# Grouping the attention work of chunks 4 to 7 into pairs, and four slices of the second token group on 512 tokens

## The chip, the core and the metric

One core of a Trainium2 chip runs the kernel. The metric is the device time of one execution in microseconds (us). The engines are named as in the profile: PE (TensorE: matmuls, and PEld its weight loads), DVE (VectorE), ACT (ScalarE), POOL (GpSimd), SP (SyncE, which here only issues transfers).

## What is computed

Sliding-window causal attention (window 64, 8 batches, 8 heads, 576 tokens, head size 64), whose output goes through a gated feed-forward block:

```
scores = scale * q @ k^T ; mask = (0 <= rel < 64) ; attn = softmax(scores)
x = (attn @ v), reshaped to 4608 tokens x 512
out = (silu(x @ w_gate) * (x @ w_val)) @ w_out      # 512 -> 1536 -> 512
```

## The kernel before

**Tiling.** The 4608 tokens are 36 chunks of 128 tokens and 9 groups of 512 tokens (four chunks each). A chunk's attention is three steps. Scores: PE multiplies keys and queries (64-row matmuls, lines 661 and 665), ACT takes the exponential into `pt` (line 673), and DVE multiplies by the window's mask (`Sm`, lines 723 and 725). AV: PE multiplies `pt` with the values, which carry a column of ones, so that the row sums come out as well. Normalization: DVE takes reciprocals of the sums (line 807) and multiplies (line 810) into `xb`. Then `xb` is transposed to `xT`: for the early chunks by PE (line 980) with a copy from PSUM by ACT or DVE (`X`), later by a DMA on SP.

**The feed-forward part.** A group of 512 tokens has 12 slices F of 128 hidden units. A slice is four matmuls with `Wg` and four with `Wv` (line 1055), a tanh on ACT (`sig`, line 1062) and two DVE operations (`uu`, line 1064, and `hT`, line 1066). Behind the 12 slices stand four outputs O (12 matmuls each with `Wo`, line 1087; ACT copies the result out of PSUM). A slice can also be made of halves: `F1.0-1a` is slices 0 and 1 of group 1 on its first 256 tokens, `F1.10a` slice 10 alone on these; `b` is the second 256 tokens. The first 256 tokens need the `xT` of two chunks, a slice on 512 tokens that of four.

**Two forms of AV.** A query block of 64 tokens needs the keys of its own and of the preceding 64-token block. The form A (`AVs`, line 791) contracts over 128 rows in one matmul. For that, the values of the two key blocks must lie on the 128 partitions in the right halves; for every chunk but the first this takes a copy `vs` of values whose halves are put in by two copies, `H` or `h` (`shift`; 64 rows each, on ACT or POOL). There are three `vs` buffers; `VS` names the buffer of each chunk (chunk 3 has buffer 2, and so have chunks 4 and 6; chunk 5 has buffer 1, chunk 7 buffer 0). The form B (`AVmm`, line 762) contracts over 64 rows and needs no copy; the word `B4` in the order puts the scores of chunk 5 between the two halves of chunk 4's AV and then adds the normalization of chunk 4 and the mask of chunk 5.

**The order.** It is written out by hand. `EARLY` is the order of the work up to group 2; each word records operations, and each engine executes its own in the order of recording. A dependency on another engine becomes a semaphore wait in front of the instruction, behind which that engine's queue stands still. The words: `F`, `O`, `X` as above; `k2t`, `q3t`: PE transposes the keys or queries of two chunks, ACT (for half of k2t DVE) copies them out; `S4`: scores, exponentials and mask; `S4u`: the same without the mask, which the word `m4` records later; `A5`: AV in form A; `N5`: its normalization; `H4.1.1/act`: copy half 1 of the values of chunk 4 into buffer 1, on ACT. `LOADS` is the order of the DMAs that POOL issues, with POOL's own copies (`h6.1.0`) among them; a word of it is recorded as soon as its `ready` condition holds, and stops all words behind it until then. `SHIPS` is the order on SP. PSUM has eight banks; the recorder gives each step the free bank that by its own estimate is ready first.

In the kernel before, chunks 4 to 7 go so: S4 | F0.8 | B4 (with S5) | F0.9 | X4, k3t, A5 | F0.10 | X5, q3t | F0.11 | S6 | two slice pairs | B6 (with S7) | two slice pairs | X6, A7 | slices 8 to 10 on 256 tokens | X7 | slice 11 on 256 tokens, and then the second 256 tokens of group 1, with S8 and S9 in one block, and O0.0.

Of the kernel before, what the change touches and what calls it, by code (L numbers as in the profile page):

```python
# [32 lines left out]
class _Graph:  # L33
# [13 lines left out]
    def ready(self, k):  # L47
        return max((o.end for o in self.writers.get(k, []) + self.readers.get(k, [])), default=0.0)
# [294 lines left out]
class _Kernel:  # L343
# [14 lines left out]

    VS = (0, 0, 1, 2, 2, 1, 2, 0)
    EARLY = """  # L360
        V F0.4 F0.5 F0.6 k2t q2t F0.7 S4 F0.8 H4.1.1/act H5.0.1/act B4 F0.9 X4/act k3t A5 N5 F0.10 X5/act q3t F0.11 S6
        F1.0-1a F1.2-3a B6 F1.4-5a F1.6-7a X6/act A7 N7 F1.8-9a F1.10a X7/act F1.11a F1.0-1b F1.2-3b F1.4-5b F1.6-7b
        S8 S9 F1.8-9b F1.10-11b O0.0 O0.1 P8 m10 O0.2 m11 O0.3 P10 m12 O1.0 X10/act X11/act m13 O1.1 F2.0 F2.1 F2.2
        F2.3 F2.4 P12 F2.5 m14 F2.6 m15 F2.7 O1.2 P14 F2.8 m16 F2.9 m17 F2.10 F2.11 O1.3 K O2.0
    """
    LOADS = """
        k2.2 q2.2 Wg8-10 Wv8-10 v4 v5 k3.2 Wg10-12 Wv10-12 q3.2 v6 v7 k8 q8 k9 q9 Wo0-6 k10 q10 k11 q11 Wo6-12 v8 h6.1.0
        h7.0.0 v9 k12 q12 k13 q13 v10 v11 k14@O0.2 q14 k15 q15 v12 v13 k16 q16 k17 q17 v14 k18 q18 v15 k19 q19 q20 v16
        v17 k20@F2.9 q21@F2.9 k21@F2.9 q22@F2.9 v18@F2.9 v19@F2.9 k22@F3.4 q23@F3.4 k23@F3.4 q24@F3.4 v20@F3.4 v21@F3.4
        k24@O2.3 q25@O2.3 k25@O2.3 q26@O2.3 v22@O2.3 v23@O2.3 k26@O3.1 q27@O3.1 k27@O3.1 q28@O3.1 v24@O3.1 v25@O3.1  # L370
        k28@O3.3 q29@O3.3 k29@O3.3 q30@O3.3 v26@O3.3 v27@O3.3 k30@O4.1 q31@O4.1 k31@O4.1 q32@O4.1 v28@O4.1 v29@O4.1
# [790 lines left out]
    def ready(self, t):  # L1162

        d = self.did
        w, n = t[0], int(re.search(r"\d+", t).group())
        if w == "W":
            return True
        if w in "kq" and t.endswith(".2"):
            return n < 2 or w + "%dT" % (n - 2) in d
        if w in "kq":  # L1170
            return n < 16 or "T%s%d" % (w, n - 8) in d
        if w == "v":
            return n < self.NV or {"a%d" % (n - self.NV), "a%d" % (n - self.NV + 1)} <= d
        if w == "h":
            return {"v%d" % n, "V"} | ({"a3"} if t in ("h5.1.2", "h6.0.2") else set()) <= d
        if w == "x":
            c = n // 4
            return "a%d" % n in d and (c < self.NX or self.steps[c - self.NX] == NF * 512)
        x = t[1]
        return x + "%d" % n in d and (n < 8 or {"s%d" % (n - 8), "s%d" % max(0, n - (9 if x == "q" else 7))} <= d)  # L1180
# [279 lines left out]
```

## Time and profile before

| | us |
|---|---|
| three runs, median (lowest, highest) | 328.25 (326.68, 329.33) |
| profiled execution, own time | 327.04 |
| profiled execution, span | 325.2 |
| PE busy in the span | 315.4 (97%) |
| DVE, ACT, POOL busy | 205.3, 135.9, 109.8 |

A row of a timeline reads: start in us, duration in us (for several merged instructions from the first start to the last end), engine, line, operation, what it writes and reads, the tile of the array that a matmul uses, shapes, how often, and in brackets the idle time of that engine just before with the engine that ended it. Matmuls are pipelined: one issues 0.2 us after another, though each is given a longer duration; so the time of a group is read from its start to the start of the next group. Some records are missing in a trace: where a row of four matmuls shows "x3", its first start is one matmul too late.

### The profile page before, as it was taken

How to read it: one execution, taken by the hardware profiler on the slowest of the kernel's cores; microseconds unless marked ns; L12 is line 12 of the kernel's file. 1: busy time of each engine (PE TensorE's matmuls, PEld its weight loads, DVE VectorE, ACT ScalarE, POOL GpSimd, SP SyncE). 2: the span in 40 equal slices, each digit the busy share in tenths (PEclk: the TensorE clock that was granted, in tenths of full speed). 3: DMA queues.
4: the chain of work that ended last, by engine and by line, in shares of the span. 5: the costliest groups of instructions: out<-in, count | busy, mean ns of one | idle time of the engine just before them, and what ended most of it. 6: DMA issues, size and time to landing. Idle time of an engine off the chain costs nothing.

```text
span 325.2 us, 8029 instructions
## 1 busy us (share of the span) xinstructions
PE 315.4 (97%) x3417; PEld 170.2 (52%) x3452; DVE 205.3 (63%) x360; ACT 135.9 (42%) x244; POOL 109.8 (34%) x138
## 2 busy tenths in 40 slices
PE   7899999999999999999999999999999999999996
PEld 6585578855455445545444454545454544444443
DVE  4678978745387737665757575766656564854610
ACT  3734864534445236343434342525252522322322
POOL 8899990007930702406060607070502000000000
PEclk9999999999999999999999999999999999999999
DMA  9999999999999994969998999999996200201012
GB/s 139 180 186 168 170 174 134 141 136 128 147 155 154 106 171 107 145 149 155 160 164 147 163 130 126 135 120 127 125 120 80 67 34 32 69 34 38 32 64 100
DMA packets 165563, 39.93 MB, mean 123 GB/s; under 512 B 152848, under 2 KB 160784, under 8 KB 165520
## 3 DMA queue, kind: packets, MB, share of 16 engines
q0 software_dynamic: 115152, 18.62, 80.6%
q1 hardware_dynamic: 45040, 11.22, 25.9%
q10 hardware_dynamic: 5328, 9.51, 8.3%
q8 instruction: 29, 0.48, 0.6%
q14 instruction: 14, 0.11, 0.1%
HBM read 37.75 MB, written 9.44 MB: 145 GB/s over the span
## 4 chain that ended last, share of the span: by engine, by line
PE 93%; ACT 2%; DMA 2%; issue 1%; DVE 0%; POOLq 0%
PE ps L1055 57%; PE ps L1087 28%; PE ps L840 2%; DMA qs<-in_q_dram 2%; ACT pt L673 2%; PE ps L698 1%; PE ps L661 1%; PE ps L1120 1%; ACT pt L710 1%; PE ps L980 1%; PE ps L605 1%; PE ps L665 1%; PE ps L791 0%; PE ps L608 0%; PE ps L702 0%
## 5 line engine op out<-in xcount | busy, mean ns | idle before, releaser
L1055 PE MATMUL ps<-xT,Wv 128*128 128x512 bf16 (+1 forms) x487 | 110.5, 351 | 0.5
L1055 PE MATMUL ps<-xT,Wg 128*128 128x512 bf16 (+1 forms) x478 | 107.5, 351 | 2.6 <-issue 1.4
L1064 DVE SCALAR_TENSOR_TENSOR uu<-sig,ps 128x512 bf16<-128x512 bf16 (+1 forms) x109 | 74.0, 679 | 53.4 <-ACT sig L1062 52.5
L1062 ACT ACTIVATE sig<-ps 128x512 bf16<-128x512 f32 (+1 forms) x109 | 64.9, 597 | 80.5 <-PE ps L1055 79.3
L1087 PE MATMUL ps<-Wo,hT 128*128 128x512 bf16 x413 | 94.5, 379 | 0.6 <-ACT pt L673 0.3
L1066 DVE SCALAR_TENSOR_TENSOR hT<-uu,ps 128x512 bf16<-128x512 bf16 (+1 forms) x109 | 74.3, 682 | 3.8
L1055 PEld LDWEIGHTS ps<-xT,Wv 128*128 128x128 bf16 x496 | 48.5, 98 | 44.9
L551 POOL DMA_DIRECT2D kn<-in_k_dram x31 | 29.4, 953 | 123.6 <-PE ps L1087 94.0
L1055 PEld LDWEIGHTS ps<-xT,Wg 128*128 128x128 bf16 x496 | 46.6, 98 | 41.6 <-ACT pt L673 0.2
L1087 PEld LDWEIGHTS ps<-Wo,hT 128*128 128x128 bf16 x420 | 40.9, 98 | 48.7
L1094 ACT ACTIVATE ost<-ps 128x512 f32<-128x512 f32 x35 | 20.9, 597 | 89.1 <-PE ps L1087 83.1
L551 POOL DMA_DIRECT2D va<-in_v_dram x40 | 36.2, 964 | 12.3 <-PE ps L1087 12.3
L551 POOL DMA_DIRECT2D qn<-in_q_dram x31 | 29.7, 969 | 0.0
L867 DVE RECIPROCAL rr<-ps 128x14 f32<-128x14 f32 (+1 forms) x28 | 5.7, 204 | 36.1 <-PE ps L840 35.9
L673 ACT ACTIVATE pt<-ps 128x512 bf16<-128x512 f32 x36 | 18.8, 598 | 4.8 <-PE ps L665 4.6
L869 DVE TENSOR_TENSOR xb<-ps,rr 128x896 bf16<-128x896 f32 (+1 forms) x28 | 19.4, 691 | 1.0
L710 ACT ACTIVATE pt<-ps 128x512 bf16<-128x512 f32 x36 | 18.6, 603 | 2.3 <-PE ps L702 2.1
L840 PEld LDWEIGHTS ps<-va,pt 64*64 64x64 bf16 x888 | 10.8, 107 | 6.1 <-issue 5.9
L840 PE MATMUL ps<-va,pt 64*64 64x65 bf16 x888 | 13.4, 193 | 0.1
L725 DVE TENSOR_TENSOR pt<-pt,kmask 128x1024 bf16<-128x1024 bf16 x18 | 12.3, 684 | 0.0
L725 DVE TENSOR_TENSOR pt<-pt,mask 128x1024 bf16<-128x1024 bf16 x13 | 8.8, 686 | 0.8 <-ACT pt L673 0.8
L1130 DVE COPY ost<-ps 128x128 f32<-128x128 f32 x1 | 0.3, 293 | 11.8 <-PE ps L1120 11.8
(75 smaller groups left out, 151.7 us busy)
## 6 DMA issues: line engine op xcount, KB each, us to landing
out_dram<-ost ACTq DMA_DIRECT2D x35, 256.0 KB, 3.0
va<-in_v_dram POOLq DMA_DIRECT2D x32, 128.0 KB, 6.7
kn<-in_k_dram POOLq DMA_DIRECT2D x25, 128.0 KB, 5.4
qn<-in_q_dram POOLq DMA_DIRECT2D x25, 128.0 KB, 5.5
Wg<-in_moe_w_gate_dram POOLq DMA_DIRECT2D x6, 256.0 KB, 7.4
Wv<-in_moe_w_val_dram POOLq DMA_DIRECT2D x6, 256.0 KB, 7.4
Wo<-in_moe_w_out_dram POOLq DMA_DIRECT2D x2, 768.0 KB, 18.9
qs<-in_q_dram POOLq DMA_DIRECT2D x3, 256.0 KB, 6.9
```

What stands on the lines that cost most here:

```text
L551: self.g.op("pool", lambda e, d=d, a=a: e.dma_start(d, a), writes=ks, dma=True, after=self.hold)
L673: g.op("act", lambda e, po=po, p=p: e.activation(po, sv[p], ACTF.Exp, scale=SCALE), reads=[bx[p][1]], writes=[pk[p]])
L710: g.op("act", lambda e, po=po, p=p: e.activation(po, sv[p], ACTF.Exp, scale=SCALE), reads=[bx[p][1]], writes=[pk[p]])
L725: self.g.op("dve", lambda e: e.tensor_tensor(pt, pt, m, ALU.mult), reads=pk + [key], writes=pk)
L840: z = e.matmul(self.psa[64 * c:64 * c + 64, o:o + 65], pt[p][rows, h, 64 * a:64 * a + 64], va[m][rows, h, 0:65], start=first, stop=phase = ...
L869: g.op("dve", lambda e, d=d, num=num, rb=rb: e.tensor_tensor(d, num, rb, ALU.mult), reads=bk + [("rr", n + k)], writes=xk, cost=(1.0, 0.25 ...
L1055: r = e.matmul(bank[:, a * n:a * n + n], W[:, kk, f * 128:f * 128 + 128], xT[:, kk, lo:hi], start=(kk == 0), stop=(kk == NK - 1))
L1062: g.op("act", lambda e, G=bank: e.activation(sig[:, 0:w], G[:, 0:w], ACTF.Tanh, scale=0.5), reads=[bk], writes=[("sig", i)])
L1064: g.op("dve", lambda e: e.scalar_tensor_tensor(uu[:, 0:w], sig[:, 0:w], 1.0, G[:, 0:w], ALU.add, ALU.mult), reads=[("sig", i), gk], writes ...
L1066: g.op("dve", lambda e: e.scalar_tensor_tensor(out, v3(uu), 0.5, v3(V), ALU.mult, ALU.mult), reads=[("uu", i), vk], writes=[("hT", ih, f) ...
L1087: r = e.matmul(OB[:, :], hT[:, f, 128 * u:128 * u + 128], self.Wo[:, f, :], start=(f == 0), stop=(f == NF - 1), skip_group_check=mid is no ...
L1094: g.op("act", lambda e: e.activation(ost[:, :], OB[:, :], ACTF.Copy), reads=[ok], writes=[("ost", io)])
```

## The change

Chunks 4 and 5, and then 6 and 7, are taken together. The scores of two chunks stand in one block (`S4u S5u`), their masks are recorded behind the slice that follows (`m4 m5` behind F0.8, `m6 m7` behind F1.0-1a), and their AVs, all in form A, stand in one block one slice later (`A4 A5 N4 N5`). X4 and X5 go together behind q3t, X5's copy moves from ACT to DVE, X6 and X7 go together in front of F1.8. Slices 8 to 11 of group 1 are taken on 512 tokens in place of two halves of 256. S8 and S9 keep their distance of two slice pairs from O0.0.

The form A of chunks 4 and 6 needs four more copies: h3.1.2 (POOL, between the loads of v5 and k3), H4.0.2 (ACT), and h5.1.2 and h6.0.2 (POOL). The last two stand, with h6.1.0 and h7.0.0, in front of the load of k10, and are recorded once `a4` is done, since they overwrite the buffer that A4 reads.

```diff
     EARLY = """
-        V F0.4 F0.5 F0.6 k2t q2t F0.7 S4 F0.8 H4.1.1/act H5.0.1/act B4 F0.9 X4/act k3t A5 N5 F0.10 X5/act q3t F0.11 S6
-        F1.0-1a F1.2-3a B6 F1.4-5a F1.6-7a X6/act A7 N7 F1.8-9a F1.10a X7/act F1.11a F1.0-1b F1.2-3b F1.4-5b F1.6-7b
-        S8 S9 F1.8-9b F1.10-11b O0.0 O0.1 P8 m10 O0.2 ...
+        V F0.4 F0.5 F0.6 k2t q2t F0.7 S4u S5u F0.8 H4.0.2/act H4.1.1/act H5.0.1/act m4 m5 F0.9 A4 A5 N4 N5 k3t F0.10 q3t
+        X4/act X5/dve F0.11 S6u S7u F1.0-1a m6 m7 F1.2-3a A6 A7 N6 N7 F1.4-5a F1.6-7a X6/act X7/act F1.8 F1.9 F1.10 F1.11
+        F1.0-1b F1.2-3b
+        S8 S9 F1.4-5b F1.6-7b O0.0 O0.1 P8 m10 O0.2 ...
     LOADS = """
-        k2.2 q2.2 Wg8-10 Wv8-10 v4 v5 k3.2 Wg10-12 Wv10-12 q3.2 v6 v7 k8 q8 k9 q9 Wo0-6 k10 q10 k11 q11 Wo6-12 v8 h6.1.0
-        h7.0.0 v9 k12 ...
+        k2.2 q2.2 Wg8-10 Wv8-10 v4 v5 h3.1.2 k3.2 Wg10-12 Wv10-12 q3.2 v6 v7 k8 q8 k9 q9 Wo0-6 h5.1.2 h6.0.2 h6.1.0 h7.0.0 k10
+        q10 k11 q11 Wo6-12 v8 v9 k12 ...
         if w == "h":
-            return {"v%d" % n, "V"} | ({"a3"} if t in ("h5.1.2", "h6.0.2") else set()) <= d
+            return {"v%d" % n, "V"} | ({"a4"} if t in ("h5.1.2", "h6.0.2") else set()) <= d
```

More of the change, by code (lines that the diff above doesn't have):

```diff
@@ L360 @@
     EARLY = """
-        V F0.4 F0.5 F0.6 k2t q2t F0.7 S4 F0.8 H4.1.1/act H5.0.1/act B4 F0.9 X4/act k3t A5 N5 F0.10 X5/act q3t F0.11 S6
-        F1.0-1a F1.2-3a B6 F1.4-5a F1.6-7a X6/act A7 N7 F1.8-9a F1.10a X7/act F1.11a F1.0-1b F1.2-3b F1.4-5b F1.6-7b
-        S8 S9 F1.8-9b F1.10-11b O0.0 O0.1 P8 m10 O0.2 m11 O0.3 P10 m12 O1.0 X10/act X11/act m13 O1.1 F2.0 F2.1 F2.2
+        V F0.4 F0.5 F0.6 k2t q2t F0.7 S4u S5u F0.8 H4.0.2/act H4.1.1/act H5.0.1/act m4 m5 F0.9 A4 A5 N4 N5 k3t F0.10 q3t
+        X4/act X5/dve F0.11 S6u S7u F1.0-1a m6 m7 F1.2-3a A6 A7 N6 N7 F1.4-5a F1.6-7a X6/act X7/act F1.8 F1.9 F1.10 F1.11
+        F1.0-1b F1.2-3b
+        S8 S9 F1.4-5b F1.6-7b O0.0 O0.1 P8 m10 O0.2 m11 O0.3 P10 m12 O1.0 X10/act X11/act m13 O1.1 F2.0 F2.1 F2.2
         F2.3 F2.4 P12 F2.5 m14 F2.6 m15 F2.7 O1.2 P14 F2.8 m16 F2.9 m17 F2.10 F2.11 O1.3 K O2.0
@@ L366 @@
     LOADS = """
-        k2.2 q2.2 Wg8-10 Wv8-10 v4 v5 k3.2 Wg10-12 Wv10-12 q3.2 v6 v7 k8 q8 k9 q9 Wo0-6 k10 q10 k11 q11 Wo6-12 v8 h6.1.0
-        h7.0.0 v9 k12 q12 k13 q13 v10 v11 k14@O0.2 q14 k15 q15 v12 v13 k16 q16 k17 q17 v14 k18 q18 v15 k19 q19 q20 v16
+        k2.2 q2.2 Wg8-10 Wv8-10 v4 v5 h3.1.2 k3.2 Wg10-12 Wv10-12 q3.2 v6 v7 k8 q8 k9 q9 Wo0-6 h5.1.2 h6.0.2 h6.1.0 h7.0.0 k10
+        q10 k11 q11 Wo6-12 v8 v9 k12 q12 k13 q13 v10 v11 k14@O0.2 q14 k15 q15 v12 v13 k16 q16 k17 q17 v14 k18 q18 v15 k19 q19 q20 v16
         v17 k20@F2.9 q21@F2.9 k21@F2.9 q22@F2.9 v18@F2.9 v19@F2.9 k22@F3.4 q23@F3.4 k23@F3.4 q24@F3.4 v20@F3.4 v21@F3.4
```

## Prediction

> **What bounds the kernel now.** I read the page's shares first, then its chain of waits, then the list of waits of the early part, then the timelines of PE, ACT and DVE around the change.
>
> ```profile
> PE 315.4 (97%) x3417; PEld 170.2 (52%) x3452; DVE 205.3 (63%) x360; ACT 135.9 (42%) x244; POOL 109.8 (34%) x138
> PE 93%; ACT 2%; DMA 2%; issue 1%; DVE 0%; POOLq 0%
> ...
> PE ps L1055 <- issue: 0.3, 2, 0.2
> ...
> PE ps L1055 <- issue: 1.1, 7, 0.2
> ```
>
> PE is busy for 97% of the span and makes 93% of the chain that ends last. The two last rows are the longest waits of PE from 28 to 66 us (the stretch that the change touches) and from 66 us to the end. Even these are mostly records that are missing, not waits. So in the changed stretch PE never stands still, and behind it there is no slack in which a delay could vanish: what PE gains or loses there arrives at the end in full. The question is what PE's blocks cost, and whether the new order makes PE wait.
>
> **What PE's blocks cost.** The timeline of PE, first and last rows of each block:
>
> ```profile
> 31.05 1.03 PE L1055 MATMUL ps<-xT,Wv 128*128 128x512 bf16 x4
> 32.61 0.81 PE L1055 MATMUL ps<-xT,Wg 128*128 128x512 bf16 x3 [0.16 <-issue]
> 33.26 1.03 PE L1055 MATMUL ps<-xT,Wv 128*128 128x512 bf16 x4
> 35.09 0.81 PE L1055 MATMUL ps<-xT,Wg 128*128 128x512 bf16 x3 [0.16 <-issue]
> 36.60 0.39 PE L980 MATMUL ps<-ident,xb 128*128 128x128 bf16 x4
> 36.82 0.61 PE L605 MATMUL ps<-ident,ks 128*128 128x128 bf16 x8
> 37.36 0.22 PE L791 MATMUL ps<-vs,pt 128*64 128x65 bf16 x1
> 37.74 1.04 PE L1055 MATMUL ps<-xT,Wg 128*128 128x512 bf16 x4
> 41.01 1.03 PE L1055 MATMUL ps<-xT,Wv 128*128 128x512 bf16 x4
> 42.34 1.05 PE L1055 MATMUL ps<-xT,Wg 128*128 128x256 bf16 x8
> 44.97 1.04 PE L1055 MATMUL ps<-xT,Wv 128*128 128x256 bf16 x8
> 46.59 1.05 PE L1055 MATMUL ps<-xT,Wg 128*128 128x256 bf16 x8
> 50.09 0.39 PE L980 MATMUL ps<-ident,xb 128*128 128x128 bf16 x4
> 50.79 1.05 PE L1055 MATMUL ps<-xT,Wg 128*128 128x256 bf16 x8
> 60.63 1.04 PE L1055 MATMUL ps<-xT,Wv 128*128 128x256 bf16 x8
> 62.22 1.05 PE L1055 MATMUL ps<-xT,Wg 128*128 128x256 bf16 x8
> ```
>
> The unit prices: from 32.61 to 33.26 three matmuls of 512 columns issue, 0.217 each (a slice of eight: 1.73). From 46.59 to 50.09 stand 32 of 256 columns, 0.1094 each (two slices on 256 tokens: 1.75). Four transposes take 36.82 - 36.60 = 0.22. The rows with x3 lack their first record, so these groups begin 0.22 earlier, at 32.39 and 34.87.
>
> A block's cost is the start of the next group less the end of issue of the group before:
> - S4: 32.39 - (31.05 + 0.87) = 0.47. B4 with S5: 34.87 - (33.26 + 0.87) = 0.74. A5: 37.74 - (36.82 + 0.44) = 0.48. S6: 42.34 - (41.01 + 0.87) = 0.46. B6 with S7: 46.59 - (44.97 + 0.875) = 0.74. A7: 50.79 - (50.09 + 0.22) = 0.48. Together 3.37.
> - After: two blocks of two scores. The block of S8 and S9 is this: 62.22 - (60.63 + 0.875) = 0.72. And two blocks of two AVs in form A. A5's matmuls start 0.10 behind the transposes and hand over 0.38 later; of this about 0.28 is work (the 16 matmuls) and 0.10 the change of shape. Two AVs: 0.10 + 0.28 + 0.28 + 0.10 = 0.76. Together 2 x (0.72 + 0.76) = 2.96. **Gain 0.41.** The pair of AVs has no row; its ends are 0.56 (no change of shape at all) and 0.96 (two blocks), so the gain lies between 0.0 and 0.8.
> - Slices 8 to 11 of group 1: 64 matmuls of 0.1094 become 32 of 0.217: 7.00 - 6.94 = **gain 0.06**.
> - Transposes (X4 to X7, k3t, q3t): the same number, no difference. The copy that moves from ACT to DVE (X5) and the two added copies on ACT and POOL lie beside PE; whether they make it wait is the next part.
>
> So with no new wait PE would gain 0.47.
>
> **Which waits are new.** Both queues, ACT's and DVE's, are served in order, and the change puts more in front of what PE needs. The prices:
>
> ```profile
> 31.25 0.60 ACT L1062 ACTIVATE sig<-ps 128x512 bf16<-128x512 f32 x1
> 37.52 1.08 ACT L478 ACTIVATE kT<-ps 128x512 bf16<-128x512 bf16 x2
> 50.52 0.60 ACT L478 ACTIVATE xT<-ps 128x512 bf16<-128x512 bf16 x1 [0.50 <-PE ps L980]
> 62.08 2.06 ACT L673 ACTIVATE pt<-ps 128x512 bf16<-128x512 f32 x4 [0.66 <-PE ps L665]
> 64.00 0.63 ACT L1062 ACTIVATE sig<-ps 128x512 bf16<-128x512 f32 x1
> ...
> 31.88 0.69 DVE L1064 SCALAR_TENSOR_TENSOR uu<-sig,ps 128x512 bf16<-128x512 bf16 x1 [0.61 <-ACT sig L1062]
> 32.63 0.69 DVE L1066 SCALAR_TENSOR_TENSOR hT<-uu,ps 128x512 bf16<-128x512 bf16 x1
> 33.23 0.80 DVE L723 TENSOR_TENSOR pt<-pt,mask 128x512 bf16<-128x512 bf16 x2
> 47.97 0.68 DVE L725 TENSOR_TENSOR pt<-pt,mask 128x1024 bf16<-128x1024 bf16 x1
> ...
> 8.24 0.69 DVE L480 COPY qT<-ps 128x512 bf16<-128x512 bf16 x1 [1.26 <-PE ps L608]
> ...
> 8.98 0.24 PE L661 MATMUL ps<-qT,kT 64*64 64x128 bf16 x2 [0.25 <-DVE qT L480]
> ...
> 71.00 0.44 PE L840 MATMUL ps<-va,pt 64*64 64x65 bf16 x30
> ```
>
> Call E the end of issue of the slice in front of a block of two scores. At S8 and S9 E is 61.50, the four exponentials begin at 62.08 (E + 0.58), and the next tanh begins behind them at 64.00 (E + 2.50). From a tanh's start to `uu` are 0.63 (31.25 to 31.88), to `hT` 0.75 more, to the next DVE operation 0.60 more. So a mask that is recorded behind the next slice starts at E + 4.48, though its exponentials were ready long before; before, chunk 4's mask stood in front of the next slice's `uu` (33.23, one operation behind `hT` of F0.7). A mask of 1024 columns ends after 0.68 and lets the next start after 0.60 like `hT`; chunk 4's, in two parts, ends after 0.80. A matmul that waits for DVE starts 0.05 behind the end of the operation (8.93 to 8.98).
>
> 1. *A4 and A5.* PE is there at E + 0.72 + 3.47 (F0.8, F0.9) = E + 4.19 and without a wait would be through at E + 4.95. But m4 ends at E + 5.28, m5 at E + 5.88; A5 starts at E + 5.93 and hands over 0.38 later, at E + 6.31. **Wait 1.4.** Behind A5 in PE's queue stand k3t and F0.10, which need nothing of it and are held all the same.
> 2. *A6 and A7.* PE is there at E + 0.72 + 3.50, would be through at E + 4.98. m6 runs from E + 4.48, m7 from E + 5.08 to E + 5.76; A7 starts at E + 5.81 and is through at E + 6.19. **Wait 1.2.** F1.4-5a is queued behind it.
> 3. *F1.8.* On 512 tokens it needs the `xT` of chunks 6 and 7, whose transposes stand right in front of it (before, slices on the first 256 tokens stood between). From the start of the transposes to the first copy are 50.52 - 50.09 = 0.43, two copies on ACT take 1.08, the hand-over 0.05: 1.56, of which PE's eight transposes cover 0.44. **Wait 1.1.** Every later matmul is queued behind it.
>
> Each wait has a row for every term; its unknown is what an engine does in between, so I give each 0.3 either way. I looked for more: k3t, q3t, X4, X5, S6, F1.0-1a and the banks of PSUM come out ready before PE arrives, because PE is late itself by then (X5 closest, by some 0.2). ACT's added copy H4.0.2 (about 0.5, one of a pair like that at 37.52) delays F0.9's tanh, whose `uu` stands behind m5 on DVE anyway. DVE's copy for X5 (at most the 0.69 of the copy at 8.24) ends before S6 and S7 do, in front of F1.0-1a.
>
> On POOL the four copies stand in front of k10, and h5.1.2 must wait for A4:
>
> ```profile
> 28.97 2.36 POOL L551 DMA_DIRECT2D va<-in_v_dram  x2
> 34.97 1.55 POOL L551 DMA_DIRECT2D kn<-in_k_dram  x1
> 40.88 1.26 POOL L480 COPY vs<-va 64x512 bf16<-64x512 bf16 x2
> 42.09 0.88 POOL L551 DMA_DIRECT2D va<-in_v_dram  x1
> ...
> va<-in_v_dram POOLq DMA_DIRECT2D x2, 128.0 KB, 10.9
> ...
> kn<-in_k_dram POOLq DMA_DIRECT2D x1, 128.0 KB, 17.1
> ...
> va<-in_v_dram POOLq DMA_DIRECT2D x1, 128.0 KB, 25.7
> ```
>
> v6 and v7, issued from 28.97 on, land 10.9 later, at 39.9 and about 40.7. A4 is done at 37.6. So the copies of v6 and v7 end near 41.8 (0.63 each), and k10 is issued there in place of 34.97, 6.8 later, with all loads behind it. I cost this at nothing: k10 landed 17.1 behind its issue, at 52.1, since the transfers in front of it filled the queue; issued at 41.8 it still has 10 us of queue in front of it, so SP's transposes of it, queued until it lands, keep their times. The copy h3.1.2 delays the loads behind it by 0.6, and the last of these shown, v6, waits 10.9 in the queue.
>
> **Sum.** -0.47 + 1.4 + 1.2 + 1.1 = +3.2 (bounds +2.0 to +4.4: three waits with 0.3 each, the gain between 0.1 and 0.9). The profiled execution took 327.04 (span 325.2), so 330.2 (span 328.4). It lies 1.2 below the median of the three runs, and from the median the sum is 331.4. I have no reason to take either as the typical one and forecast the middle, **330.8**.
>
> **Rivals.**
> - *Only F1.8 waits* (the masks are earlier than I make them: it takes 1.4 less on ACT and DVE, as if the tanh of the next slice ran ahead of the exponentials). -0.47 + 1.1 = +0.6: 327.7, or 328.9 from the median. Against it: 64.00 behind 62.08 is the same order of queue with the same four exponentials. 12%.
> - *No wait at all, faster*: the changes of array shape that go are the whole effect, and PE's run-ahead covers the masks and copies. -0.47: 326.6. It decides only if the three waits together stay under 0.47, and they come to 3.7 by rows. 5%.
> - *The loads come late.* If the queue runs dry while POOL stands at h5.1.2, all loads shift by 6.8. v9 landed at 42.09 + 25.7 = 67.8 and would land at 74.6. The first AV that reads it (71.00 in PE's timeline) comes at 74.2: 0.4 late; a load without any slack now would be 6.8 - 3.2 = 3.6 late. Taking 2: 332.8. For it: nothing is issued for 7 us; against it the 17.1. 10%.
> - *The clock of PE falls.* In the row below PE had 3.5 us of gaps in 16.6 and was still granted 1.00. If the three waits drop the clock all the same, and one 512-token slice behind each runs at half rate, 3 x 1.73 = 5.2 come on top: 336.0. 6%.
>
> ```profile
> 0.00:16.60 16.60, 13.06 (x327) 9.53 (x328) 9.28 (x29) 9.03 (x16) 14.15 (x24) 1.00 1.46 160
> ```
>
> [...]
>
> **How the numbers follow.** The forecast has 64%, the rivals 12, 5, 10 and 6, and 3 are left for what I don't see. A measurement of this kernel can tell about 1%, 3.3 us, from no change, and the forecast's +3.2 lies on that bound. Half of its chance counts as slower: 32 + 10 + 6, with 1 of the rest, 49%. Within 1%: 32 + 12 + 5, 49%. Faster by over 1%: 2%. The range: the forecast's bounds are 327.04 + 2.0 and 328.25 + 4.4, 329.0 to 332.7; with half of the first rival and the late loads, and without no wait and the clock, **328.3 to 334.0**.
>
> **What would show it.** In the profile after, waits of PE of about 0.5 to 1.1 on DVE's masks in front of A4 and A5 and of A6 and A7, and 1.1 on ACT's copy in front of F1.8; a block of two AVs of 0.76 and of two scores of 0.72 where nothing waits; the first matmul of O0.0 3.2 later than before; k10 landing at 52 as before. The forecast is wrong if PE's total of waits between 28 and 70 us is under 2, if a load ends a wait of PE behind 66 us, or if the granted clock leaves 1.00.

## The result, and the profile after

| | us |
|---|---|
| kernel after, six runs, median (lowest, highest) | 330.09 (329.79, 334.19) |
| kernel before, six runs beside them | 327.26 (326.57, 329.33) |
| ratio of the times | 1.0118, 95% interval 1.0076 to 1.016 |
| profiled execution after, own time and span | 329.79 and 328.1 |

The forecast was 330.8 with a range of 328.3 to 334.0. The time is 0.7 below the forecast and inside the range. The ratio lies a little above the 1% that the forecast took as its bound, but only because two of the six runs of the kernel after took 334 us: the medians are 2.83 us apart (0.9%), and in e8 below, where no run was that long, the ratio is 1.0086.

The line numbers of the kernel after are one higher than before. From its page, the busy times and the chain that ended last; then the list of PE's waits from 28 to 70 us:

```profile
PE 315.7 (96%) x3353; PEld 167.2 (51%) x3388; DVE 205.0 (62%) x359; ACT 135.7 (41%) x243; POOL 111.4 (34%) x141
...
PE 90%; ACT 4%; DVE 2%; DMA 2%; issue 2%; POOLq 0%
```

```profile
PE ps L1056 <- ACT xT L479: 1.2, 1, 1.2
PE ps L792 <- DVE pt L726: 1.2, 3, 0.8
PE ps L792 <- DVE pt L724: 1.0, 1, 1.0
```

PE is as busy as before (315.7 for 315.4 us), but the span is 2.9 longer. The three points lost by PE in the chain went mostly to ACT and DVE, and the list names them: 3.4 us of waits, where the largest entry before was 0.3. They show up one by one in PE's timeline:

```profile
30.73 1.03 PE L1056 MATMUL ps<-xT,Wv 128*128 128x512 bf16 x4
32.54 0.81 PE L1056 MATMUL ps<-xT,Wg 128*128 128x512 bf16 x3 [0.16 <-issue]
34.91 1.03 PE L1056 MATMUL ps<-xT,Wv 128*128 128x512 bf16 x4
36.89 0.22 PE L792 MATMUL ps<-vs,pt 128*64 128x65 bf16 x1 [0.95 <-DVE pt L724]
37.49 0.22 PE L792 MATMUL ps<-vs,pt 128*64 128x65 bf16 x1 [0.16 <-DVE pt L726]
37.87 0.62 PE L606 MATMUL ps<-ident,ks 128*128 128x128 bf16 x8
...
41.81 1.03 PE L1056 MATMUL ps<-xT,Wv 128*128 128x512 bf16 x4
...
47.91 0.22 PE L792 MATMUL ps<-vs,pt 128*64 128x65 bf16 x1 [0.84 <-DVE pt L726]
48.51 0.22 PE L792 MATMUL ps<-vs,pt 128*64 128x65 bf16 x1 [0.16 <-DVE pt L726]
48.88 1.05 PE L1056 MATMUL ps<-xT,Wg 128*128 128x256 bf16 x8
...
52.39 0.61 PE L981 MATMUL ps<-ident,xb 128*128 128x128 bf16 x8
54.18 0.81 PE L1056 MATMUL ps<-xT,Wg 128*128 128x512 bf16 x3 [1.18 <-ACT xT L479]
...
68.81 5.13 PE L1088 MATMUL ps<-Wo,hT 128*128 128x512 bf16 x23
```

The same point before:

```profile
65.94 5.13 PE L1087 MATMUL ps<-Wo,hT 128*128 128x512 bf16 x23
```

To compare kernels without their start-up, which differs by some tenths from execution to execution, I take the *stretch*: from the start of F0.7's matmuls with `Wv` to the first recorded matmul of O0.0. Before it is 65.94 - 31.05 = 34.89 us, after 68.81 - 30.73 = 38.08: **3.19 longer**, where the forecast had 3.2. (Both rows lack the first of the 24 matmuls of O0.0 and O0.1, so the difference is not touched by it. The spans differ by 0.3 less, because the profiled execution of the kernel after reached F0.7 0.32 sooner.) Behind it PE waits no more than before; the first row of its waits from 66 us to the end is the same:

```profile
PE ps L1056 <- issue: 1.1, 7, 0.2
```

Why the masks are late is seen on ACT and on DVE:

```profile
32.17 2.07 ACT L674 ACTIVATE pt<-ps 128x512 bf16<-128x512 f32 x4 [0.65 <-PE ps L666]
34.09 0.63 ACT L1063 ACTIVATE sig<-ps 128x512 bf16<-128x512 f32 x1
```

```profile
34.76 0.69 DVE L1065 SCALAR_TENSOR_TENSOR uu<-sig,ps 128x512 bf16<-128x512 bf16 x1 [1.77 <-ACT sig L1063]
35.48 0.69 DVE L1067 SCALAR_TENSOR_TENSOR hT<-uu,ps 128x512 bf16<-128x512 bf16 x1
36.08 0.75 DVE L724 TENSOR_TENSOR pt<-pt,mask 128x512 bf16<-128x512 bf16 x2
36.75 0.69 DVE L726 TENSOR_TENSOR pt<-pt,mask 128x1024 bf16<-128x1024 bf16 x1
```

DVE stands idle for 1.77 us for F0.8's tanh, which comes behind four exponentials on ACT. The masks stand behind F0.8 in DVE's queue, so DVE does not use that time for them although the first exponentials are done: in e1 below, where they stand ahead of F0.8, both are done before PE comes to the AVs. The mask m4 starts at 36.08; E, the end of issue of F0.7, is 30.73 + 0.87 = 31.60, so this is E + 4.48, as forecast.

### The profile page after: what moved, and what is told of

It is laid out like the page before. It is cut to its first block, busy times and chain, and to the rows that moved or that the text cites. A ratio compares the mean times of both kernels' runs of the same rounds, so it can differ in the third digit from the quotient of the medians.

```text
span 328.1 us, 7893 instructions
## 1 busy us (share of the span) xinstructions
PE 315.7 (96%) x3353; PEld 167.2 (51%) x3388; DVE 205.0 (62%) x359; ACT 135.7 (41%) x243; POOL 111.4 (34%) x141
## 3 DMA queue, kind: packets, MB, share of 16 engines
HBM read 37.75 MB, written 9.44 MB: 144 GB/s over the span
## 4 chain that ended last, share of the span: by engine, by line
PE 90%; ACT 4%; DVE 2%; DMA 2%; issue 2%; POOLq 0%
PE ps L1056 54%; PE ps L1088 28%; ACT pt L674 3%; PE ps L841 2%; DMA qs<-in_q_dram 2%; PE ps L1121 1%; PE ps L662 1%; PE ps L699 1%; DVE pt L726 1%; PE ps L606 1%; ACT pt L711 1%; PE ps L981 1%; PE ps L792 0%; PE ps L666 0%; DVE uu L1065 0%
## 5 line engine op out<-in xcount | busy, mean ns | idle before, releaser
L1065 DVE SCALAR_TENSOR_TENSOR uu<-sig,ps 128x512 bf16<-128x512 bf16 x108 | 73.8, 684 | 57.0 <-ACT sig L1063 56.2
L1063 ACT ACTIVATE sig<-ps 128x512 bf16<-128x512 f32 x108 | 64.7, 601 | 83.7 <-PE ps L1056 82.6
L1067 DVE SCALAR_TENSOR_TENSOR hT<-uu,ps 128x512 bf16<-128x512 bf16 x108 | 74.2, 687 | 3.8
L1056 PEld LDWEIGHTS ps<-xT,Wv 128*128 128x128 bf16 x480 | 47.0, 98 | 46.4
L552 POOL DMA_DIRECT2D kn<-in_k_dram x31 | 27.4, 890 | 122.2 <-PE ps L1088 92.3
L1056 PEld LDWEIGHTS ps<-xT,Wg 128*128 128x128 bf16 x480 | 45.3, 98 | 44.3 <-ACT xT L479 1.1
L552 POOL DMA_DIRECT2D va<-in_v_dram x40 | 35.2, 931 | 12.4 <-PE ps L1088 12.3
L552 POOL DMA_DIRECT2D qn<-in_q_dram x31 | 27.7, 905 | 0.0
```

Of the source, the lines that this page charges most:

```text
L552: self.g.op("pool", lambda e, d=d, a=a: e.dma_start(d, a), writes=ks, dma=True, after=self.hold)
L1056: r = e.matmul(bank[:, a * n:a * n + n], W[:, kk, f * 128:f * 128 + 128], xT[:, kk, lo:hi], start=(kk == 0), stop=(kk == NK - 1))
L1063: g.op("act", lambda e, G=bank: e.activation(sig[:, 0:w], G[:, 0:w], ACTF.Tanh, scale=0.5), reads=[bk], writes=[("sig", i)])
L1065: g.op("dve", lambda e: e.scalar_tensor_tensor(uu[:, 0:w], sig[:, 0:w], 1.0, G[:, 0:w], ALU.add, ALU.mult), reads=[("sig", i), gk], writes ...
L1067: g.op("dve", lambda e: e.scalar_tensor_tensor(out, v3(uu), 0.5, v3(V), ALU.mult, ALU.mult), reads=[("uu", i), vk], writes=[("hT", ih, f) ...
```

## The experiments

Times of one table row are from one chip, beside runs of the kernel before there. The stretch is from the profiled execution.

| run | median (lowest, highest) | ratio to before, 95% interval | stretch less that of before |
|---|---|---|---|
| kernel after | 330.09 (329.79, 334.19) | 1.0118, 1.0076 to 1.016 | +3.19 |
| e1_masks_first | 328.25 (327.98, 334.93) | 1.0044, 1.0027 to 1.0061 | +1.37 |
| e2_filler | 329.07 (328.67, 329.17) | 1.0068, 1.0053 to 1.0083 | +2.10 |
| e3_both | 327.14 (326.92, 327.35) | 1.0005, 0.9986 to 1.0024 | +0.28 |
| e4_pool_late | 330.4 (329.61, 334.52) | 1.013, 1.0088 to 1.0173 | +3.18 |
| e5_late_mask_before | 329.04 (328.71, 331.84) | 1.0088, 1.006 to 1.0117 | |
| e6_own_rows_on_dve | 327.14 (326.67, 328.19) | 0.9992, 0.9965 to 1.0019 | |
| e7_no_idle | 330.32 (329.75, 335.08) | 1.0093, 1.006 to 1.0126 | |
| e8_after_again | 329.85 (329.65, 329.93) | 1.0086, 1.0053 to 1.0118 | |
| e9_shifted_fetch | 329.56 (329.29, 331.0) | 1.0075, 1.0049 to 1.01 | |
| e10_own_rows_on_pool | 326.85 (326.08, 329.66) | 1.0001, 0.9973 to 1.0029 | -0.19 |

### The masks ahead of the slices

```diff
-F0.7 S4u S5u F0.8 H4.0.2/act H4.1.1/act H5.0.1/act m4 m5 F0.9 A4 A5
+F0.7 S4u S5u m4 m5 F0.8 H4.0.2/act H4.1.1/act H5.0.1/act F0.9 A4 A5
-S6u S7u F1.0-1a m6 m7 F1.2-3a
+S6u S7u m6 m7 F1.0-1a F1.2-3a
```

> The changed kernel with m4 m5 recorded in front of F0.8 and m6 m7 in front of F1.0-1a, so that DVE masks before it does the slice's two operations. Theory (the masks stood in DVE's queue behind a slice whose tanh stood behind four exponentials): m5 and m7 end about E + 3.4, before PE has done the two slices (E + 4.2), so the waits in front of A4/A5 (1.4) and A6/A7 (1.2) go and the one in front of F1.8 (1.1) stays: 2.6 less than the changed kernel, about 0.6 over the kernel before (ratio 1.002). Rival (the loads that POOL issues 6 us later cost the time): no change, ratio 1.009 to 1.012. Rival (the exponentials on ACT are themselves too late): the waits before A5 and A7 stay, ratio 1.006 or more.

Both waits on masks went, and the stretch became 1.82 shorter, 0.7 less than the waits had been worth. PE's list of waits (and two rows of its timeline) shows what came in their place, and the timelines of ACT and DVE show where from:

```profile
PE ps L1056 <- ACT xT L479: 1.2, 1, 1.2
PE ps L1056 <- DVE uu L1065: 0.4, 1, 0.4
PE ps L792 <- ACT vs L479: 0.2, 1, 0.2
...
36.54 0.22 PE L792 MATMUL ps<-vs,pt 128*64 128x65 bf16 x1 [0.23 <-ACT vs L479]
37.97 0.81 PE L1056 MATMUL ps<-xT,Wg 128*128 128x512 bf16 x3 [0.43 <-DVE uu L1065]
```

```profile
34.56 1.92 ACT L479 ACTIVATE vs<-va 64x512 bf16<-64x512 bf16 x3
36.39 0.57 ACT L1063 ACTIVATE sig<-ps 128x512 bf16<-128x512 f32 x1
```

```profile
37.00 0.69 DVE L1065 SCALAR_TENSOR_TENSOR uu<-sig,ps 128x512 bf16<-128x512 bf16 x1 [0.73 <-ACT sig L1063]
```

The three value copies on ACT, one of which the change added, end at 36.48. A5 needs the third, and F0.9's tanh is queued behind all three, at 36.39; its `uu` ends at 37.69, and F0.10 waits for it. In the kernel after PE stood still for the masks at that time, so these two waits cost nothing there. The theory missed them. The list gives them as 0.2 and 0.4, because it counts from the modelled end of the matmul before. By starts each is 0.4: A5's first matmul comes at 36.54 in place of 36.14, and F0.10, whose first record is missing, at 37.75 in place of 37.35. Together that is the 0.7 within 0.1.

### A slice between the transposes and the 512-token slices

```diff
-X6/act X7/act F1.8 F1.9 F1.10 F1.11
+X6/act X7/act F1.8-9a F1.10 F1.11
-S8 S9 F1.4-5b F1.6-7b O0.0
+S8 S9 F1.4-5b F1.6-7b F1.8-9b O0.0
```

> The changed kernel with a slice pair on the first 256 tokens (F1.8-9a) between X7 and the first slice on 512 tokens; its second half comes behind F1.6-7b. Theory (F1.8 waits for ACT's two copies of xT): 1.1 less than the changed kernel, since the filler lasts 1.75, about 2.1 over the kernel before (ratio 1.006); the waits before the AVs stay. Rival (loads): no change, ratio 1.009 to 1.012.

The wait on ACT's copies went, with nothing in its place, and the stretch is 1.09 shorter. F1.8-9a needs only the first 256 tokens, whose `xT` was ready long before, and covers the two copies.

### Both edits

> Both edits together. Theory: no wait of PE of over 0.2 between 28 and 70 us, and what is left is the gain of fewer blocks: 0.4 to 0.5 below the kernel before (ratio 0.9985), 3.7 below the changed kernel; the stretch from the last slice in front of S4 to O0.0 takes 33.3 in place of 33.8 before. Rival (the clock or the tile shape costs time by itself): the stretch takes 33.8 or more though nothing waits. Rival (loads): ratio 1.009 or more.

The stretch is 2.91 shorter than in the kernel after, just the sum of the two edits (1.82 and 1.09), so the waits are independent of each other. But the expected gain over the kernel before did not come: the two waits of the first run are here too, again 0.4 each by starts (A5 at 36.64 in place of 36.24, F0.10 at 37.85 in place of 37.46). These 0.8, less the gain of PE's blocks of about 0.5, leave 0.3, and the stretch is 0.28 longer than before.

### POOL's copies later

```diff
-... Wo0-6 h5.1.2 h6.0.2 h6.1.0 h7.0.0 k10 q10 k11 q11 Wo6-12 v8 v9 ...
+... Wo0-6 k10 q10 k11 q11 Wo6-12 v8 h5.1.2 h6.0.2 h6.1.0 h7.0.0 v9 ...
```

> The changed kernel with POOL's four copies (h5.1.2, h6.0.2, h6.1.0, h7.0.0) behind the load of v8, where two of them stood before, so that k10 and the loads behind it are issued near 35 us again. Theory (the stand of POOL costs nothing): same time as the changed kernel within 0.3, all three waits of PE stay. Rival (loads): 0.4 to 3 less than the changed kernel.

The stretch is the same within 0.01. So POOL's stand in front of h5.1.2 costs nothing, as forecast: in the kernel after k10 is issued at 41.26 and lands 10.5 later, at 51.8 (52.1 before).

```profile
41.26 0.88 POOL L552 DMA_DIRECT2D kn<-in_k_dram  x1
```

```profile
kn<-in_k_dram POOLq DMA_DIRECT2D x1, 128.0 KB, 10.5
```

The profiled execution of this run has a wait of another kind, at 106.8 us; it is told below with e7.

### A late mask in the kernel before

```diff
-F0.7 S4 F0.8 H4.1.1/act H5.0.1/act B4 F0.9
+F0.7 S4u F0.8 H4.1.1/act H5.0.1/act m4 B4 F0.9
```

> The kernel before with one edit: the mask of chunk 4 is issued on VectorE behind the two operations of F0.8 instead of ahead of them; the pairs of blocks, the slices and everything else stay as before. Theory: the price of the first wait comes from the place of the mask in VectorE's queue and not from the pairing. F0.8's tanh stands behind the two exps of chunk 4 on ACT, so its two VectorE operations end some 3.6 us after the score block's start and the mask 0.7 later, at about 4.3, while TensorE comes to chunk 4's AVs 2.3 us after it: a wait of 2.0 us on the mask ahead of the AVs, and about 328.7 us, 2.1 over the kernel before. Rival, in which it is the pairing that costs: no wait above 0.5 us, and the time of the kernel before within 0.4 us.

The median is 2.3 over the kernel before and the profiled execution, at 328.75, 2.0 over it; three of the eight runs, from 330.2 to 331.8, had a mean granted clock of 0.995. PE waits 2.0 us in one place that did not exist before:

```profile
PE ps L762 <- DVE pt L723: 2.0, 1, 2.0
```

```profile
34.04 0.69 DVE L1064 SCALAR_TENSOR_TENSOR uu<-sig,ps 128x512 bf16<-128x512 bf16 x1 [0.80 <-ACT sig L1062]
34.76 0.69 DVE L1066 SCALAR_TENSOR_TENSOR hT<-uu,ps 128x512 bf16<-128x512 bf16 x1
35.37 0.75 DVE L723 TENSOR_TENSOR pt<-pt,mask 128x512 bf16<-128x512 bf16 x2
```

So it is the mask's place in DVE's queue that costs, in a kernel without the change's pairs. The wait is longer than in the pair because only one slice stands between scores and AVs here: behind the end of issue of F0.7, PE arrives after 0.47 + 1.73 = 2.20 in place of 4.19, while the mask, with two exponentials ahead of the tanh and not four, ends after 36.12 - 31.86 = 4.26 in place of 36.83 - 31.60 = 5.23.

### The copies on DVE, then on POOL

Two runs tried to free ACT of the copies behind the two small waits of the first and third run: H4.0.2 and H4.1.1 on DVE in front of the masks (e6), and only H4.0.2 on POOL, in front of the issue of Wo's first half (e10). Both start from the kernel with both edits.

```diff
-S4u S5u m4 m5 F0.8 H4.0.2/act H4.1.1/act H5.0.1/act F0.9
+S4u S5u H4.0.2/dve H4.1.1/dve m4 m5 F0.8 H5.0.1/act F0.9      # e6
+S4u S5u m4 m5 F0.8 H4.0.2/pool H4.1.1/act H5.0.1/act F0.9     # e10, with Wo0-6 held until it
```

> The kernel after with both edits of the third run (masks ahead of the slices, a slice as filler ahead of the 512-token slices), and in addition the copies H4.0.2 and H4.1.1 on VectorE ahead of the two masks, where VectorE has nothing to do, so that ACT has only the copy H5.0.1 behind F0.8's tanh. Theory: what kept the third run from a gain are two small waits (0.4 on F0.9's VectorE operation, whose tanh stood behind three copies on ACT, and 0.2 on the third copy); with two of the three copies off ACT both go, and the time is 0.4 to 0.6 us under that run's, 326.6, or 0.1 to 0.5 under the kernel before. Rival, in which the pairing gains nothing by itself: the waits go and the time stays at that of the third run, 327.1, because the blocks cost as much as before.

> The kernel of the third run (masks ahead of the slices, a slice as filler) with the copy H4.0.2 on POOL, ahead of the issue of Wo's first half, instead of on ACT; on VectorE it had cost 0.97 us for each copy and had pushed F0.8's operations, on whose bank the AVs then waited 1.3 us. Theory: POOL has issued q9 by 34.8, 1.1 us before TensorE comes to chunk 4's AVs, and takes 0.6 for the copy; ACT has two copies ahead of F0.9's tanh instead of three, so the waits of 0.4 (F0.9's VectorE operation) and 0.2 (third copy) go and nothing takes their place: 0.5 to 0.6 us under that run, a ratio of 0.9985 to the kernel before. Rival, in which the pairing has no gain of its own: a ratio of 1.0005 as in that run, with the waits gone or moved.

On DVE the profile shows the theory failing: the two small waits went, but the two copies took 1.85 us, the masks and F0.8's operations came later, and the AVs of chunk 5 waited 1.3 us for F0.8's `hT`, which reads a PSUM bank (that A5 takes this bank is inferred from the wait). But the profiled execution, at 328.19, is the longest of the eleven, 1.05 over their median, so how much of this wait the usual run has is not shown; and by the times (ratio 0.9992, 0.9965 to 1.0019) neither the theory nor its rival can be told. The two rows are from PE's waits and DVE's timeline of e6:

```profile
PE ps L792 <- DVE hT L1067: 1.3, 1, 1.3
```

```profile
33.54 1.85 DVE L481 COPY vs<-va 64x512 bf16<-64x512 bf16 x2
```

On POOL it held in part. No wait of PE is left in the list but missing records; the stretch is 0.47 under that of e3 and 0.19 under that of the kernel before. From PE's timeline of e10, first the one gap that remains, between A4 and A5, and then the blocks without any wait:

```profile
36.50 0.20 PE L792 MATMUL ps<-vs,pt 128*64 128x65 bf16 x1
36.81 0.19 PE L792 MATMUL ps<-vs,pt 128*64 128x65 bf16 x1
...
41.16 1.03 PE L1056 MATMUL ps<-xT,Wv 128*128 128x512 bf16 x4
42.75 1.05 PE L1056 MATMUL ps<-xT,Wg 128*128 128x256 bf16 x8
...
45.38 1.04 PE L1056 MATMUL ps<-xT,Wv 128*128 128x256 bf16 x8
46.98 1.05 PE L1056 MATMUL ps<-xT,Wg 128*128 128x256 bf16 x8
```

The pair of scores takes 42.75 - (41.16 + 0.87) = 0.72, the pair of AVs 46.98 - (45.38 + 0.875) = 0.725. The gap of 0.28 (0.31 between two matmuls that otherwise start 0.03 apart) ends at 36.81, 0.14 after F0.8's `hT` on DVE does (35.98 + 0.69), the same 0.14 as in e6 (38.22 behind 38.08), so it is most likely a remainder of that wait; a run that takes it away was not made. In the whole time, 0.19 cannot be told from nothing (ratio 1.0001, 0.9973 to 1.0029): no version was measurably faster than the kernel before.

### Is it PE's standing still that gives the runs of 334 us?

The two runs of the kernel after at 334 us had a mean granted clock of 0.995. The forecast had such a case as a rival: the new waits drop the clock. In e7 PE works through the wait ahead of F1.8; the waits on the masks stay.

```diff
-X6/act X7/act F1.8 F1.9
+X6/act X7/act Y F1.8 F1.9        # Y: self.warm(5) on a free PSUM bank
```

> The kernel after with five matmuls of 512 columns on zeros put between the transposes of X7 and the first 512-token slice, in a PSUM bank that nothing reads: about 1.07 us of work in the place where TensorE waited 1.2 us for the copies of X6 and X7; nothing else is changed and nothing is computed with them. Both theories: the slice starts when the copies are done, so the usual time is that of the kernel after, 330.1 within 0.3 us. They differ in the runs of 334 us at a granted clock of 0.995, which were 5 of 18 with the 1.2 us wait and none of 16 without: if TensorE standing still behind the transposes lowers the clock, none of these runs is above 332; if it is the lateness or the chip, about 3 of 11 are.

> The kernel after, unchanged, beside the run with the five matmuls on the same chip. 330.1 us in most runs; by the theory that TensorE's stand ahead of F1.8 lowers the clock, about 3 of 11 runs come out at 334 us with a clock of 0.995; by the rival, as many as of the kernel with the matmuls.

The usual time was as expected, but two of the six runs of e7 were at 333.7 and 335.1, and none of the four of e8 was over 330. The theory that the wait ahead of F1.8 lowers the clock fell. The profiled execution of e7 was one of those of 334 us (own time 333.69, clock 0.995), and shows the place. Windows of it (us, then busy time with count of PE, PEld, DVE, ACT and POOL, the granted clock, DMA share, GB/s):

```profile
52.00:54.00 2.00, 2.00 (x19) 1.25 (x17) 1.93 (x4) 1.47 (x3) 1.39 (x2) 1.00 1.88 158
54.00:56.00 2.00, 2.00 (x11) 0.92 (x11) 0.43 (x2) 0.60 (x1) 0.00 (x0) 1.00 1.31 205
...
106.00:108.00 2.00, 0.68 (x71) 0.58 (x59) 0.00 (x0) 1.93 (x5) 0.00 (x0) 1.00 1.62 49
108.00:110.00 2.00, 1.20 (x10) 0.56 (x10) 0.87 (x2) 0.34 (x1) 0.00 (x0) 0.79 0.35 73
110.00:112.00 2.00, 2.00 (x6) 0.76 (x5) 1.43 (x4) 0.60 (x1) 0.00 (x0) 0.50 0.00 0
112.00:114.00 2.00, 2.00 (x10) 0.82 (x8) 1.38 (x3) 0.53 (x1) 0.15 (x1) 0.85 0.62 127
```

```profile
106.31 0.37 PE L841 MATMUL ps<-va,pt 64*64 64x65 bf16 x21
108.80 0.26 PE L841 MATMUL ps<-va,pt 64*64 64x65 bf16 x7 [2.12 <-issue]
```

At F1.8 the clock is 1.00. At about 106.7 us, long behind the change, PE stops for 2.12 us in the middle of a row of AV matmuls, with no engine and no transfer of data as the releaser, and then runs at half the clock: 0.79, 0.50 and 0.85 in three rows of 2 us are worth about 3.4 us at a half. In the profiled execution of e4 (own time 332.15) it stops in the same row for 2.08, and the clock stays at 1.00:

```profile
108.84 0.22 PE L841 MATMUL ps<-va,pt 64*64 64x65 bf16 x2 [2.08 <-issue]
```

### Where the stop comes from

Among the DMA queues the trace has one called "instruction", with packets of 16384 bytes, 28 of them in the kernel after, 3 to 19 us apart. Its rows in windows of 1 us (packets, MB, time as a share of 16 engines): in e8, which does not stop, from 104 to 105 us; in e7 from 105 to 106; in e4 from 106 to 107.

```profile
q8 instruction: 1, 0.02, 5.9%
```

```profile
q8 instruction: 1, 0.02, 12.4%
```

```profile
q8 instruction: 1, 0.02, 8.6%
```

By the trace's own times the packet runs from 104.31 to 105.26 in e8 (and from 103.89 to 104.84 in the kernel after), from 105.41 to 107.40 in e7, and from 106.11 to 107.48 in e4. In the last two PE goes on 1.4 us behind its end, at 108.80 and 108.84; in the first two it was there before PE came to 106.7. For which engine a single packet is, the trace does not say. PE has 3353 + 3388 of the 7893 recorded instructions of the kernel after, so my estimate is that most of the 28 packets are PE's. My reading of e4 and e7 is that these two are, and that PE ran out of instructions there. The test takes 64 matmuls and their weight loads, 128 instructions, out of PE's stream ahead of that place. If a packet comes at a fixed place of the stream, it then stands elsewhere in the work, and the stop should leave this row of AV matmuls, with no run above 332 us and a usual time of 330.1 within 0.5:

```diff
-        self.warm(92, n=52)
+        self.warm(28, n=171)
```

> The kernel after with one edit: the 92 warm-up matmuls of 52 columns at the very start are 28 of 171 columns, the same number of columns (4788 for 4784) with 64 matmuls and their weight loads fewer, so that what follows stands 128 instructions earlier in TensorE's stream. In the profiled run with the five matmuls TensorE stopped for 2.1 us in the middle of a row of AV matmuls at 106.7 us, where the trace names no releaser, a 16 KB transfer of the instruction queue had begun at 105.4 where the kernel after begins it at 103.9 to 104.3, and the clock was at a half for 4 us behind the stop. [...] Rival (the lateness, or chance of the chip): as in the kernels with the 3 us before this, in which 8 of 28 runs came out between 332 and 335 us, about 3 of 11 do so here, with the stop at the same matmul.

In the profile a packet of the instruction queue begins between 101 and 102 us, where in the kernel after none begins between 96.58 and 103.89. No run of twelve is above 331.0, and the profile has no stop. By itself this is not proof, since it could come by chance: with the 8 of 28 of the expectation it would do so about once in sixty times (0.714 to the twelfth power). Also, e9 ran on another chip than e1, e4, e7 and e8, with no run of the kernel after beside it, and the four runs of e8 had no long one without the edit. Together with the two late packets, that PE ran out of instructions in e4 and e7 is the most likely reading, but it is not shown: no run delays or advances that packet alone. That the two runs of 334 us of the kernel after, of which there is no profile, had the same stop is argued, not shown. Nor is it a property of the kernel after alone: beside e9 and e10 two of 23 runs of the kernel before were at 333.1 and 333.7, and their cause is not shown.

## Why the prediction was right, point by point

| step | forecast | measured |
|---|---|---|
| pair of scores | 0.72 | 0.72 |
| pair of AVs | 0.76 | 0.725 (second pair of e10) |
| gain of the blocks | 0.41 | 0.48 |
| m4 starts at | E + 4.48 | E + 4.48 |
| wait at A4 and A5 | 1.4 | 1.3 |
| wait at A6 and A7 | 1.2 | 1.2 |
| wait at F1.8 | 1.1 | 1.13 |
| POOL's stand | 0 | 0 (e4) |
| first matmul of O0.0 | +3.2 | +3.19 |

- **The sum.** The waits by the timeline above: k3t at 37.87 in place of E + 4.95 = 36.55; F1.4-5a at 48.88 in place of 42.68 + 4.98 = 47.66 (E of the second pair is 41.81 + 0.87); at F1.8 the list's 1.18 has to be corrected, since its first record is missing: it starts at 54.18 - 0.22 = 53.96, and the transposes' issue ends at 52.39 + 0.44 = 52.83, which makes 1.13. Together 3.67, less the gain of 0.48 + 0.06: 3.13, where the stretch shows 3.19. The steps were sized from rows of the kernel before, above all from the block of S8 and S9, which was already ordered as the new ones would be, and none is off by more than 0.1. Blocks: 3.37 - 2 x (0.72 + 0.725) = 0.48. The 0.10 for a change of the array's shape was a little too large: with the same 0.28 for a chunk's matmuls, the pair of AVs leaves 0.725 - 0.56 = 0.165 for both ends, 0.08 each. The bounds of the sum were added up a little too narrow: with the forecast's own terms (3.7, 0.3 for each wait, a gain from 0.1 to 0.9) they are +1.9 and +4.5, not +2.0 and +4.4.
- **The base.** The total was 0.7 over, and the step that did it was the choice of the middle between the profiled execution's 327.04 and the median of three runs, 328.25. The median of six runs is 327.26 and, on other chips, 326.65 to 326.83: the profiled execution was the typical one. From it the sum is 330.2, and 330.09 was measured. That this fits within 0.1 is partly luck: the profiled execution lies 0.2 under the median of the six, and by the medians the change is 2.8, not 3.2.
- **The wrong rivals.** "Only F1.8 waits" and "no wait" needed the tanh to be early; ACT's rows show it behind the exponentials. "The loads come late" fell with e4. "The clock falls": through the three waits (0.95, 0.84 and 1.18 in PE's rows) it stays at 1.00 in the profile after, from 31.6 to 68.6 us. No run shows the half rate that this rival was costed with behind any of them; a clock of 0.50 is shown only in e7, behind its stop of 2.12 us. The runs of 334 us that look like this rival go with a stop in another place, as far as a profile shows it (e7), and none of them is in the forecast: I had called a granted clock off 1.00 a sign of error, and in two of six runs it was off.
- **What the forecast did not see.** It put ACT's added copy at nothing, "F0.9's tanh, whose `uu` stands behind m5 on DVE anyway". That was right for this kernel and only as long as the masks were late: with the masks first, the two waits behind ACT's three copies, 0.8 by starts, are what makes e3 no faster than the kernel before; moving this one copy to POOL (e10) took 0.47 off the stretch. The cover had to be named with its price, because an engineer who mends the waits loses it.

## What to carry to other kernels

An operation that is ready but is recorded behind one that waits (here a mask behind the followers of a tanh) can cost PE the wait (1.3 and 1.2 us at the two pairs of AVs), and three waits cost far more here (3.7) than larger blocks on PE saved (0.5). A cost that lies in the shadow of a wait comes back when the wait is mended: here three waits were worth 3.7 us, and mending them brought 2.9, so the shadows belong into the forecast of the mended version. A new block is sized best by a block of the same order elsewhere in the same trace.

## What the runs showed of the hardware that was not expected

- PE stopped for 2.08 us (e4) and 2.12 us (e7) in a block of the shortest matmuls (30 of them in a row of 0.44 us) with no releaser in the trace. In both profiles a 16 KB packet of the instruction queue ended at 107.4 to 107.5 us in place of 104.8 to 105.3; that PE ran out of instructions is my reading, which no run shows. Why the packet was late is not shown. The DMA share from 106 to 107 us is 3.04 in e7 and 2.59 in e4, against 1.66 in the kernel after and 1.59 in e8, and the queue q1 took 301.8% (as a share of 16 engines) for 376 packets in e7 and 76.9% for 422 in the kernel after, so the transfers of data took longer at that time too.
- Behind one stop of 2.12 us the clock was granted at a half for about 3.4 us (e7); behind one of 2.08 us in the same place it stayed at 1.00 (e4). The wait of 1.1 us ahead of F1.8 never lowered it in a profile. In e5, whose one wait lasts 2.0 us, three of eight runs had a mean clock of 0.995, against one of the 19 runs of the kernel before beside it. Its profile is of a run at 1.00, so where the clock fell is not shown, nor whether such a wait costs more than its own time.
- The copies of 64 x 512 values were dearest on DVE in these profiles: two took 1.85 us there (e6), three 1.92 on ACT (e1), and two 1.26 on POOL (the row of the forecast).
